# The second layer of a fused attention and MoE kernel in its loop's own order, with sums of token blocks on GpSimd

## The chip, the core and the metric

The kernel runs on one core of a Trainium2 chip. The metric is the device time of one execution in microseconds (us), as a median of several runs. The engines are TensorE (PE in the profile, its weight loads PEld), VectorE (DVE), ScalarE (ACT), GpSimd (POOL) and SyncE (SP), which here only issues transfers.

## The reference, cut to what matters

Two attentions in a row give x, 2304 tokens of 512 values. Then come two layers of matrix products:

```
h = x @ w_in                       # 512 -> 2048
x = (h * sigmoid(1.702 h)) @ w_out # 2048 -> 512          the first layer
p = probs / (probs.sum(-1) + 1e-9)
for e in range(4):                 # the second layer: 4 experts, w1[e] 512x1024, w2[e] 1024x512
    out += p[:, e] * (relu(x @ w1[e]) @ w2[e])
```

All inputs are float32. The kernel keeps the precision by splitting each operand into a rounded high part and the remainder, its low part, and adding three products of the four.

## The kernel before, in words

**Attention and the first layer** run first (up to 466 us of the profiled span). An order planned by hand covers the attention; the tail of the first layer, where the change begins, is issued by the framework's own scheduler. It steps through `moe` (eight token blocks j of 288 in the last pass, four steps c in each); after a step `moe_step` (the loop `while pos["m"] < len(moe) - CPP`) also advances what stands in the dictionary `beside` for it: there the operands of the second layer's first pair and first quad are made. PE's lines there are L500 and L528, VectorE's L520 (low part of a hidden block) and L553 (sum into the output block).

**The second layer** takes the tokens in three pairs of blocks of 2 x 384 (`NPAIR`, `TB`), and for each pair 16 **quads**: 4 experts times 4 slices of 256 hidden values, 48 quads in all. One quad computes relu(x @ w1 slice) for a whole pair by a seven-product scheme (`PRODUCTS`, L680) instead of eight products. Each product multiplies a sum of weight blocks (A11, S1 to S4, ...) by a sum of token blocks (B11, T1 to T4, ...), 6 matmuls of 128x384. What it needs:

- **Token operands**, once for a pair: `b_operand` (L593 to L615). T1 = B12-B11 and T2 = B22-T1 on VectorE (L592, L593), T3 = B22-B12 and T4 = B21-T2 on GpSimd (L597, L602), then for each of the seven names two high parts on ScalarE (L614) and two low parts, one on VectorE and one on GpSimd (L615). These take 10 buffers (28 thirds) and live through the pair's 16 quads.
- **Weight operands**, for each quad: `fetch_w1` (L622) and `fetch_w2` (L628) on SP; `w1_operand`: the sums S1 to S4 on VectorE (L649 to L653), then high parts on ScalarE and low parts on GpSimd (`split`, L153 and L154) in the order S2 S3, A11 A12, A22, S1 S4; `w2_operand` the same for two slices. Nine buffers for a quad: raw w1, the sums, four for w1's operands, raw w2, two for w2.

All of these come from one pool, `big`, with 29 buffers of equal size. A buffer is given in the order in which the kernel's text asks for it, when an older one has been read for the last time.

**A quad's loop** (the last loop of the kernel) has steps k = 0 to 7. Step k issues product k of quad n (`quad`), whose result VectorE adds up (L706, L710, L714, L715, L720) and ScalarE and VectorE turn into the two parts of a hidden block (`hidden`, L688 and L689); then one output tile of quad n-1 (`l2_second`: 6 matmuls of 128x512, L732, added up with the token's probability by VectorE, L743, in the first quad of a pair written by ScalarE, L741); then a step of the weight operands of quad n+1 and of w2 of quad n. At k = 5 the raw w2 of the next quad is asked for; in the last quad of a pair each step also makes one token operand of the next pair. An output tile that is finished is stored by SP (L747).

**What sets the order** in the kernel before: every engine runs its instructions in the order in which they stand in its queue. In the second layer and in the first layer's tail that order is not the text's but the framework scheduler's, which puts at the front what it takes to be ready first, the text's order deciding between ready ones.

Of the kernel before, what the change touches and what calls it, by code (L numbers as in the profile page):

```python
# [8 lines left out]
F32 = mybir.dt.float32  # L9
# [88 lines left out]
def packed_attention_moe_kernel(  # L98
# [13 lines left out]
    nc = tc.nc  # L112
    B, H, S, D = q.shape
# [11 lines left out]
    CPP = 4  # L125


    TB = 384
    NPAIR = NT // (2 * TB)
# [16 lines left out]
    def slot(shape, dt, name):  # L146
        return big.tile(shape, dt, tag="b", name=name)
# [17 lines left out]
    quads = [(i, e, c) for i in range(NPAIR) for e in range(NE) for c in range(w1.shape[2] // 256)]  # L165
# [413 lines left out]
    h2 = {}  # L579
    ACC2 = {}  # L580

    def b_operand(i):

        y = ACC[i]
        B = {f"B{r + 1}{b + 1}": y[:, 2 * r:2 * r + 2, b * TB:(b + 1) * TB] for r in range(2) for b in range(2)}
        parts = []
        one = two = None
        for n, name in enumerate(TOK):
            if name == "T2":
                one = slot([128, 2, TB], F32, "t1")  # L590
                two = slot([128, 2, TB], F32, "t2")
                nc.vector.tensor_sub(out=one, in0=B["B12"], in1=B["B11"])  # L592
                nc.vector.tensor_sub(out=two, in0=B["B22"], in1=one)  # L593
                src = two
            elif name == "T3":
                three = slot([128, 2, TB], F32, "t3")
                nc.gpsimd.tensor_sub(out=three, in0=B["B22"], in1=B["B12"])  # L597
                src = three
            elif name == "T1":
                src = one  # L600
            elif name == "T4":
                nc.gpsimd.tensor_sub(out=two, in0=B["B21"], in1=two)  # L602
                src = two
            else:
                src = B[name]
            for hl in range(2):
                for kk in range(2):
                    p = 4 * n + 2 * hl + kk
                    if p % 3 == 0:
                        parts.append(slot([128, 3, TB], F32R, "b"))  # L610
                    Bop[i, name, hl, kk] = parts[p // 3][:, p % 3, :]
            for kk in range(2):
                hi, lo = Bop[i, name, 0, kk], Bop[i, name, 1, kk]
                nc.scalar.copy(out=hi, in_=src[:, kk, :])  # L614
                (nc.vector, nc.gpsimd)[kk].tensor_sub(out=lo, in0=src[:, kk, :], in1=hi.bitcast(F32))  # L615
            yield

    def fetch_w1(n):
        if n < len(quads):
            i, e, c = quads[n]  # L620
            raw = raws["w1", n] = slot([128, KD, 256], F32, "raw1")
            nc.sync.dma_start(out=raw, in_=w1[e][:, c * 256:(c + 1) * 256].rearrange("(k p) f -> p k f", p=128))  # L622

    def fetch_w2(n):
        if n < len(quads):
            i, e, c = quads[n]
            raw = raws["w2", n] = slot([128, 2, 512], F32, "raw2")
            nc.sync.dma_start(out=raw, in_=w2[e][c * 256:(c + 1) * 256, :].rearrange("(c p) d -> p c d", p=128))  # L628
# [36 lines left out]
    def w2_operand(n):  # L665
        raw = raws.pop(("w2", n))
        for c in range(2):
            yield
            w = W2[n, c] = slot([128, 2, 512], F32R, "w2")
            split(w[:, 0, :], w[:, 1, :], raw[:, c, :], nc.gpsimd)  # L670
            yield
# [24 lines left out]
    def quad(n):  # L696

        for b in range(2):
            h2[n, b] = hp.tile([128, 2, 2, TB], F32R, tag="h", name=f"h{b}")
        ps = product(n, 0)  # L700
        P = f32_tile("p1")
        nc.scalar.copy(out=P, in_=ps)  # L702
        yield
        ps = product(n, 1)
        U = f32_tile("u")
        nc.vector.tensor_add(out=U, in0=ps, in1=P)  # L706
        yield
        ps = product(n, 2)
        UV = f32_tile("uv")
        nc.vector.tensor_add(out=UV, in0=ps, in1=U)  # L710
        yield
        ps = product(n, 3)
        C22 = f32_tile("c22")
        nc.vector.tensor_add(out=C22, in0=ps, in1=UV)  # L714
        nc.vector.tensor_add(out=U, in0=ps, in1=U)  # L715
        hidden(n, 1, 1, C22)
        yield
        for k, c, b, more in ((4, 0, 0, P), (5, 1, 0, UV), (6, 0, 1, U)):
            ps = product(n, k)
            nc.vector.tensor_add(out=more, in0=ps, in1=more)  # L720
            hidden(n, c, b, more)
            yield
# [33 lines left out]
    def norm_probs():  # L756
        nc.sync.dma_start(out=pr, in_=probs.rearrange("(t p) e -> p t e", p=128))
        nc.vector.reduce_sum(out=prs, in_=pr, axis=AX.X)
        nc.vector.tensor_scalar_add(prs, prs, 1e-9)
        nc.vector.reciprocal(out=prs, in_=prs)  # L760
        nc.vector.tensor_mul(out=pr, in0=pr, in1=prs.unsqueeze(2).to_broadcast([128, NT // 128, NE]))
# [4 lines left out]
    moe = [(packed_w, (0, 0), None)]  # L766
# [22 lines left out]
    pos = {"m": 0}  # L789
# [16 lines left out]
    def moe_step():  # L806
        fn, args, tag = moe[pos["m"]]
        pos["m"] += 1
        part = fn(*args)
        if part is not None:  # L810
            order.drain(part)
        due["n"] = max(due["n"], todo.get(tag, 0))
        if state["cvt"] < due["n"]:
            make_w()
        for part in beside.get(tag, ()):
            next(part, None)
# [56 lines left out]
    engines = {e.engine for e in (nc.tensor, nc.vector, nc.scalar, nc.gpsimd, nc.sync)}  # L873
    with tc.manual_schedule(engines=engines):
# [13 lines left out]
        for p in list(order.parts):  # L888
            order.finish(p)
    norm_probs()  # L890
    b_parts = {i: b_operand(i) for i in range(NPAIR)}
    last = n_pass1 - 1
    fetch_w1(0)
    fetch_w2(0)
    first = w1_operand(0)
    beside = {}
    for j in (6, 7):
        for c in range(CPP):
            beside["first", last, j - 1, c] = (b_parts[0], first)
    while pos["m"] < len(moe) - CPP:  # L900
        moe_step()
    per_pair = len(quads) // NPAIR

    for n in range(len(quads) + 1):
        none = iter(())
        now = quad(n) if n < len(quads) else none
        fetch_w1(n + 1)
        after = w1_operand(n + 1) if n + 1 < len(quads) else none
        w2_now = w2_operand(n) if n < len(quads) else none
        tiles = list(range(2 * TB // 128))  # L910
        for k in range(8):
            next(now, None)
            if k > 0:
                if n == 0:
                    if pos["m"] < len(moe):
                        moe_step()
                elif tiles:
                    l2_second(n - 1, tiles.pop(0))
            next(after, None)
            next(w2_now, None)  # L920
            if k == 5:
                fetch_w2(n + 1)
            if n % per_pair == per_pair - 1 and n // per_pair + 1 < NPAIR:
                next(b_parts[n // per_pair + 1], None)


# [28 lines left out]
```

## Time and profile before

| | |
|---|---|
| median of 3 runs | 1252.76 us (1251.65 to 1253.18) |
| the profiled execution, its own time | 1249.63 us |
| span in its profile | 1247.4 us |
| PE busy in the span | 1175.7 us, 94% |
| VectorE, ScalarE, GpSimd busy | 899.5, 523.6, 483.0 us |
| mean granted clock of TensorE | 0.967 |

The span is the time from the first to the last instruction; the execution's own time has 2.2 us more around it. In the profile "busy" is the time in which an engine works on an instruction; the square brackets at the end of a timeline row give the idle time of that engine just before it, and what ended it. In the windows' rows (x79) is a number of instructions, and PEclk is the granted share of TensorE's full clock.

### The profile page before, as it was taken

What the parts mean: (1) busy time and instruction counts of PE and PEld (TensorE: products, weight loads), DVE (VectorE), ACT (ScalarE), POOL (GpSimd) and SP (SyncE); (2) the same over time, 40 slices, a digit from 0 to 9 for tenths busy, and PEclk for the clock granted to TensorE, in tenths of its full rate; (3) what the DMA queues carried; (4) which work ended last, traced back from release to release, by engine and by line L of the source; (5) the groups of instructions that cost most, each with busy time, mean ns of one, the idle gap of its engine ahead of it and who ended that gap; (6) DMA issues with size and microseconds to landing.
All of it is one profiled execution on the core that took longest, in us unless ns stands there. A gap on an engine that the chain in (4) does not pass through costs nothing. (4 is left out here: it accounts for less than half of the span.)

```text
span 1247.4 us, 18269 instructions
## 1 busy us (share of the span) xinstructions
PE 1175.7 (94%) x6912; PEld 1062.0 (85%) x6912; DVE 899.5 (72%) x1652; ACT 523.6 (42%) x1152; POOL 483.0 (39%) x409
## 2 busy tenths in 40 slices
PE   5778788999999989999999989999999999999998
PEld 4467577999999989999999969999999789999997
DVE  4873678786875856777777876777778767777775
ACT  3567655444434634433333444333333353333321
POOL 1320023221120345544444664444444744444430
PEclk8779989999999989999999989999999899999999
DMA  8623321121110012222222132222221332222201
GB/s 234 177 76 82 85 66 54 51 69 52 51 35 18 1 51 69 68 68 69 68 68 68 34 118 69 68 68 68 68 69 41 95 119 68 68 68 68 68 18 51
DMA packets 90392, 87.46 MB, mean 70 GB/s; under 512 B 43968, under 2 KB 71616, under 8 KB 90304
## 3 DMA queue, kind: packets, MB, share of 16 engines
q1 hardware_dynamic: 90304, 86.30, 23.1%
q8 instruction: 54, 0.88, 0.3%
q14 instruction: 34, 0.28, 0.1%
HBM read 81.56 MB, written 4.72 MB: 69 GB/s over the span
## 5 line engine op out<-in xcount | busy, mean ns | idle before, releaser
L732 PE MATMUL ps_o<-w,h 128*128 128x512 f32 x1728 | 449.9, 396 | 9.7 <-ACT h L688 5.5
L680 PE MATMUL ps_p<-b,w 128*128 128x384 f32 x2016 | 402.8, 339 | 0.6 <-DVE o L743 0.6
L680 PEld LDWEIGHTS ps_p<-b,w 128*128 128x128 f32 x2016 | 362.8, 189 | 24.6 <-DVE o L743 0.9
L732 PEld LDWEIGHTS ps_o<-w,h 128*128 128x128 f32 x1728 | 323.4, 189 | 63.6 <-DVE h L689 7.2
L154 POOL TENSOR_TENSOR w<-raw,w 128x512 fp32r<-128x512 f32 x192 | 236.4, 1250 | 172.3 <-ACT w L153 170.5
L528 PE MATMUL ps_acc<-h,wout 128*128 128x288 f32 x1536 | 232.9, 300 | 6.1 <-DVE h L520 6.1
L528 PEld LDWEIGHTS ps_acc<-h,wout 128*128 128x128 f32 x1536 | 215.1, 191 | 10.0 <-DVE h L520 7.3
L743 DVE SCALAR_TENSOR_TENSOR o<-ps_o,pr,o 128x512 f32<-128x512 f32 x270 | 200.0, 741 | 5.1 <-PE ps_o L732 5.1
L154 POOL TENSOR_TENSOR w<-s,w 128x512 fp32r<-128x512 f32 x96 | 132.6, 1381 | 170.4 <-ACT w L153 170.4
L500 PE MATMUL ps_h<-a,pw 128*128 128x288 f32 x768 | 129.9, 305 | 19.1 <-ACT a L446 12.6
L153 ACT CAST w<-raw 128x512 fp32r<-128x512 f32 x192 | 106.9, 562 | 72.4 <-POOL w L154 48.0
L500 PEld LDWEIGHTS ps_h<-a,pw 128*128 128x128 f32 x768 | 113.6, 195 | 22.9 <-ACT a L446 13.4
L520 DVE TENSOR_TENSOR h<-g,h 128x288 fp32r<-128x288 f32 x128 | 73.4, 575 | 63.0 <-ACT g L517 62.0
L649 DVE TENSOR_TENSOR s<-raw 128x256 f32<-128x256 f32 x48 | 48.5, 1010 | 86.1 <-DMA raw<-in_moe_w_dram 69.8
L516 ACT ACTIVATE h<-ps_h 128x288 fp32r<-128x288 f32 x128 | 53.1, 415 | 96.5 <-PE ps_h L500 95.9
L688 ACT ACTIVATE h<-uv 128x384 fp32r<-128x384 f32 x48 | 25.2, 526 | 162.5 <-DVE uv L720 162.5
L706 DVE TENSOR_TENSOR u<-ps_p,p 128x384 f32<-128x384 f32 x48 | 26.7, 556 | 70.4 <-ACT p L702 67.2
L153 ACT CAST w<-s 128x512 fp32r<-128x512 f32 x96 | 59.1, 615 | 41.9 <-DVE s L650 19.2
L217 POOL TENSOR_SCALAR cvt<-cvt 128x512 uint32<-128x512 uint32 x32 | 23.9, 747 | 127.0 <-DVE cvt L214 108.4
L688 ACT ACTIVATE h<-c 128x384 fp32r<-128x384 f32 x48 | 25.2, 525 | 92.5 <-DVE c L714 92.5
L688 ACT ACTIVATE h<-p 128x384 fp32r<-128x384 f32 x48 | 25.2, 526 | 82.4 <-DVE p L720 82.4
L553 DVE TENSOR_TENSOR y<-ps_acc,y 128x288 f32<-128x288 f32 (+2 forms) x120 | 44.7, 388 | 11.2 <-PE ps_acc L528 11.0
(102 smaller groups left out, 1169.5 us busy)
## 6 DMA issues: line engine op xcount, KB each, us to landing
raw<-in_moe_w_dram SPq DMA_DIRECT2D x96, 512.0 KB, 3.9
raw<-in_moe_w_in_dram SPq DMA_DIRECT2D x16, 512.0 KB, 4.1
raw<-in_moe_w_out_dram SPq DMA_DIRECT2D x16, 512.0 KB, 3.8
kv<-in_k_dram SPq DMA_DIRECT2D x32, 144.0 KB, 3.3
q<-in_q_dram SPq DMA_DIRECT2D x32, 144.0 KB, 2.9
out_dram<-o SPq DMA_DIRECT2D x18, 256.0 KB, 2.0
kv<-in_v_dram SPq DMA_DIRECT2D x16, 144.0 KB, 3.0
kv<-in_v_dram SPq DMA_DIRECT2D x8, 288.0 KB, 3.5
```

What stands on the lines that cost most here:

```text
L153: nc.scalar.copy(out=hi, in_=src)
L154: eng.tensor_sub(out=lo, in0=src, in1=hi.bitcast(F32))
L500: nc.tensor.matmul(out=ps[:, :HS], lhsT=PW[a, b, g][:, wp, c * 128:(c + 1) * 128], rhs=A[b * UG + g][:, xp, s * HS:(s + 1) * HS], start=(m ...
L516: nc.scalar.activation(out=h[:, 0, :], in_=ps[:, :HS], func=AF.Gelu_apprx_sigmoid)
L520: nc.vector.tensor_sub(out=h[:, 1, :], in0=g32, in1=h[:, 0, :].bitcast(F32))
L528: nc.tensor.matmul(out=ps[:, :HS], lhsT=W["out", a, c][:, wp, t * 128:(t + 1) * 128], rhs=hid[a, j, c // 2][:, 2 * (c % 2) + hq, :], start ...
L553: nc.vector.tensor_add(out=dst, in0=src, in1=dst)
L649: nc.vector.tensor_add(out=s1, in0=Am["A21"], in1=Am["A22"])
L680: nc.tensor.matmul(out=ps, lhsT=Wop[n, a, wp, kk], rhs=Bop[i, b, xp, kk], start=(m == 0), stop=(m == 5),)
L688: nc.scalar.activation(out=h[:, 0, :], in_=src, func=AF.Relu)
L732: nc.tensor.matmul(out=ps, lhsT=h[:, c, hq, o:o + 128], rhs=W2[n, c][:, wp, :], start=(c == 0 and m == 0), stop=(c == 1 and m == 2),)
L743: nc.vector.scalar_tensor_tensor(out=acc, in0=ps, scalar=pr[:, tok, e:e + 1], in1=acc, op0=ALU.mult, op1=ALU.add,)
```

## The change

The four sums of token blocks become a generator of their own, `t_sums`, all on GpSimd and each in a buffer of its own; `b_operand` only reads them. For the first pair the steps in the first layer's tail at which sums, operands and the first quad's weights are advanced are moved: the sums beside token block 3, the weights beside 4 and 5, the operands beside 5 and 6 (before: operands and weights beside 5 and 6). For the other pairs the sums are taken in the last quad but one of the pair before (k = 0 to 3), and the operands in the last quad one step later than before (k = 1 to 7). The whole loop over quads, the last four steps of the first layer in quad 0 among it, stands in `tc.manual_schedule`: each engine issues its instructions in the order in which the text emits them.

```diff
+    Tsum = {}
+    def t_sums(i):
         y = ACC[i]
         B = {f"B{r + 1}{b + 1}": y[:, 2 * r:2 * r + 2, b * TB:(b + 1) * TB] for r in range(2) for b in range(2)}
+        for name, x, z in (("T1", "B12", "B11"), ("T2", "B22", "T1"), ("T4", "B21", "T2"), ("T3", "B22", "B12")):
+            B[name] = slot([128, 2, TB], F32, name)
+            nc.gpsimd.tensor_sub(out=B[name], in0=B[x], in1=B[z])
+            if name == "T3":
+                Tsum[i] = B
+            yield
+    def b_operand(i):
         parts = []
         for n, name in enumerate(TOK):
-            if name == "T2":
-                one = slot([128, 2, TB], F32, "t1")
-                two = slot([128, 2, TB], F32, "t2")
-                nc.vector.tensor_sub(out=one, in0=B["B12"], in1=B["B11"])
-                nc.vector.tensor_sub(out=two, in0=B["B22"], in1=one)
...
+            src = Tsum[i][name]
...
-    for j in (6, 7):
-        for c in range(CPP):
-            beside["first", last, j - 1, c] = (b_parts[0], first)
+    for c in range(CPP):
+        beside["first", last, 3, c] = (t_parts[0],)
+        beside["first", last, 4, c] = (first,)
+        beside["first", last, 5, c] = (b_parts[0], first)
+        beside["first", last, 6, c] = (b_parts[0],)
...
+    with tc.manual_schedule(engines=engines):
         for n in range(len(quads) + 1):
...
             for k in range(8):
...
-            if n % per_pair == per_pair - 1 and n // per_pair + 1 < NPAIR:
-                next(b_parts[n // per_pair + 1], None)
+                after_pair = n // per_pair + 1
+                if after_pair < NPAIR:
+                    if n % per_pair == per_pair - 2:
+                        next(t_parts[after_pair], None)
+                    if n % per_pair == per_pair - 1 and k > 0:
+                        next(b_parts[after_pair], None)
```

## Rows read from the trace of the kernel before

**Rows 1.** The page, busy time, share of the span and instructions of each engine.
```profile
PE 1175.7 (94%) x6912; PEld 1062.0 (85%) x6912; DVE 899.5 (72%) x1652; ACT 523.6 (42%) x1152; POOL 483.0 (39%) x409
```
**Rows 2.** Windows: length, busy PE, PEld, DVE, ACT, POOL, clock, DMA share, GB/s.
```profile
699.20:714.86 15.66, 15.66 (x79) 14.13 (x78) 13.46 (x19) 8.18 (x18) 12.60 (x11) 1.00 0.14 37
714.86:736.10 21.24, 18.04 (x79) 15.36 (x78) 12.62 (x24) 7.96 (x16) 14.04 (x12) 0.92 0.36 105
736.10:756.73 20.63, 17.97 (x80) 15.29 (x78) 15.14 (x26) 9.25 (x17) 9.74 (x8) 0.92 0.43 146
756.73:772.39 15.66, 15.66 (x80) 14.13 (x78) 10.88 (x18) 6.71 (x13) 7.38 (x6) 1.00 0.22 67
...
975.97:998.07 22.10, 19.32 (x79) 16.16 (x78) 14.38 (x25) 7.96 (x16) 14.69 (x12) 0.85 0.38 117
998.07:1015.79 17.72, 16.04 (x80) 13.96 (x79) 12.26 (x24) 9.04 (x17) 8.85 (x7) 1.00 0.45 148
```
**Rows 3.** Timeline of PE at the first change of pair: start, duration, what, idle before.
```profile
714.86 2.25 PE L680 MATMUL ps_p<-b,w 128*128 128x384 f32 x12
...
719.04 0.50 PE L732 MATMUL ps_o<-w,h 128*128 128x512 f32 x1 [1.47 <-DVE h L689]
```
**Rows 4.** Timeline of VectorE at the first change of pair.
```profile
695.14 2.22 DVE L689 SCALAR_TENSOR_TENSOR h<-p,h 128x384 fp32r<-128x384 f32 x1 [0.19 <-ACT h L688]
...
699.09 1.66 DVE L689 SCALAR_TENSOR_TENSOR h<-uv,h 128x384 fp32r<-128x384 f32 x1 [0.59 <-ACT h L688]
...
702.46 0.56 DVE L689 SCALAR_TENSOR_TENSOR h<-u,h 128x384 fp32r<-128x384 f32 x1 [0.59 <-ACT h L688]
...
716.76 0.43 DVE L649 TENSOR_TENSOR s<-raw 128x256 f32<-128x256 f32 x1 [1.78 <-DMA raw<-in_moe_w_dram]
```
**Rows 5.** Timeline of SP's queue at the first change of pair.
```profile
676.26 0.37 SPq L622 DMA_DIRECT2D raw<-in_moe_w_dram  x1
703.38 0.37 SPq L628 DMA_DIRECT2D raw<-in_moe_w_dram  x1
713.42 0.37 SPq L622 DMA_DIRECT2D raw<-in_moe_w_dram  x1
...
737.88 7.64 SPq L747 DMA_DIRECT2D out_dram<-o  x4
```
**Rows 6.** The page, DMA issues: the loads of w1 and w2, us to landing.
```profile
raw<-in_moe_w_dram SPq DMA_DIRECT2D x96, 512.0 KB, 3.9
```
**Rows 7.** Groups by line with shapes, whole run: busy us, mean ns of one, idle before.
```profile
L154 POOL TENSOR_TENSOR w<-raw,w 128x512 fp32r<-128x512 f32 x144 | 202.4, 1418 | 172.1 <-ACT w L153 170.2 <-PE ps_p L680 1.9
...
L153 ACT CAST w<-raw 128x512 fp32r<-128x512 f32 x144 | 87.8, 614 | 24.0 <-PE ps_p L680 15.7 <-DMA raw<-in_moe_w_dram 6.1 <-POOL w L154 2.1
...
L615 POOL TENSOR_TENSOR b<-t,b 128x384 fp32r<-128x384 f32 x12 | 13.7, 1142 | 24.7 <-PE ps_p L680 13.1 <-ACT b L614 6.1 <-DVE h L520 5.5
L741 ACT ACTIVATE o<-ps_o,pr 128x512 f32<-128x512 f32 x18 | 12.3, 681 | 0.5 <-PE ps_o L732 0.5
...
L615 DVE TENSOR_TENSOR b<-t,b 128x384 fp32r<-128x384 f32 x12 | 11.0, 919 | 0.0
...
L597 POOL TENSOR_TENSOR t<-y 128x768 f32<-128x768 f32 x3 | 5.9, 1951 | 0.0
...
L593 DVE TENSOR_TENSOR t<-y,t 128x768 f32<-128x768 f32 x3 | 2.8, 945 | 0.0
```
**Rows 8.** Timeline of GpSimd at the first change of pair.
```profile
695.10 1.85 POOL L602 TENSOR_TENSOR t<-y,t 128x768 f32<-128x768 f32 x1 [0.85 <-DVE b L615]
...
698.49 1.84 POOL L597 TENSOR_TENSOR t<-y 128x768 f32<-128x768 f32 x1
```
**Rows 9.** Windows in the first layer's last pass, columns as in rows 2.
```profile
400.00:410.00 10.00, 10.00 (x77) 10.00 (x77) 3.82 (x9) 2.85 (x8) 0.00 (x0) 1.00 0.01 2
440.00:450.00 10.00, 5.96 (x33) 5.50 (x32) 6.34 (x13) 5.41 (x14) 8.32 (x8) 0.78 0.18 54
450.00:460.00 10.00, 10.00 (x69) 10.00 (x68) 4.09 (x11) 2.35 (x7) 1.53 (x2) 0.88 0.19 52
```
**Rows 10.** Timeline of VectorE there.
```profile
444.79 0.47 DVE L649 TENSOR_TENSOR s<-raw 128x256 f32<-128x256 f32 x1 [1.80 <-DMA raw<-in_moe_w_dram]
```

More of the change, by code (lines that the diff above doesn't have):

```diff
@@ L580, in packed_attention_moe_kernel @@
     ACC2 = {}
-    def b_operand(i):
+    Tsum = {}
+    def t_sums(i):
         y = ACC[i]
         B = {f"B{r + 1}{b + 1}": y[:, 2 * r:2 * r + 2, b * TB:(b + 1) * TB] for r in range(2) for b in range(2)}
+        for name, x, z in (("T1", "B12", "B11"), ("T2", "B22", "T1"), ("T4", "B21", "T2"), ("T3", "B22", "B12")):
[5 more added lines that the diff above has]
+    def b_operand(i):
         parts = []
-        one = two = None
         for n, name in enumerate(TOK):
-            if name == "T2":
-                one = slot([128, 2, TB], F32, "t1")
-                two = slot([128, 2, TB], F32, "t2")
-                nc.vector.tensor_sub(out=one, in0=B["B12"], in1=B["B11"])
-                nc.vector.tensor_sub(out=two, in0=B["B22"], in1=one)
[L594 to L605, printed above, removed]
+            src = Tsum[i][name]
             for hl in range(2):
@@ L890, in packed_attention_moe_kernel @@
     norm_probs()
+    t_parts = {i: t_sums(i) for i in range(NPAIR)}
     b_parts = {i: b_operand(i) for i in range(NPAIR)}
@@ L902, in packed_attention_moe_kernel @@
     per_pair = len(quads) // NPAIR
[L904 to L922, printed above, removed]
-            if n % per_pair == per_pair - 1 and n // per_pair + 1 < NPAIR:
-                next(b_parts[n // per_pair + 1], None)
+    with tc.manual_schedule(engines=engines):
+        for n in range(len(quads) + 1):
+            none = iter(())
+            now = quad(n) if n < len(quads) else none
+            fetch_w1(n + 1)
+            after = w1_operand(n + 1) if n + 1 < len(quads) else none
+            w2_now = w2_operand(n) if n < len(quads) else none
+            tiles = list(range(2 * TB // 128))
+            for k in range(8):
+                next(now, None)
+                if k > 0:
+                    if n == 0:
+                        if pos["m"] < len(moe):
+                            moe_step()
+                    elif tiles:
+                        l2_second(n - 1, tiles.pop(0))
+                next(after, None)
+                next(w2_now, None)
+                if k == 5:
+                    fetch_w2(n + 1)
+                after_pair = n // per_pair + 1
[4 more added lines that the diff above has]
+                        next(b_parts[after_pair], None)
 _INS = ['q', 'k', 'v', 'p', 'moe_w_in', 'moe_w_out', 'moe2_domain_probs', 'moe2_w1', 'moe2_w2']
```

## The prediction

> **What bounds the kernel now.** I read the page's busy times first: PE works 94% of the span, nothing else above 85%, and that 85% is PE's own weight loads [rows 1]. So the question is where PE is not working. The windows answer it. I cut them at the first product of a quad, so that a row is one quad. A quad that goes well takes 15.66 us with PE busy all of it and the clock at 1.00; so do all others from the second quad on except the first two after each change of pair [rows 2]. Those four take 21.24, 20.63, 22.10 and 17.72 us: 81.69 - 4 x 15.66 = **19.05 us** lost, with the clock down to 0.92 and 0.85 in three of them [rows 2]. Everything that the change can win inside the second layer is in these four rows, since in the other quads no engine makes PE wait.
>
> What PE waits for there is the hidden block, 1.47 us at 719.04 [rows 3]; VectorE makes it late, and VectorE itself had stood 1.78 us at 716.76 for raw weights [rows 4]. The load is late because SP's queue sent nothing from 676.26 to 703.38, 27 us in which at 15.66 a quad three to four loads would go out [rows 5]. I put that down to the pool of 29 buffers: the scheduler lets the weights run more than a quad ahead, so all 29 are taken; then the next pair's ten operand buffers are asked for while the old ten live until their products in quad 15. The first load after the gap goes out when quad 15's first two products, begun at 699.20 [rows 2], have been through and free the old pair's first buffers. The trace does not show the pool, so this is my reading.
>
> A second loss lies in the first layer's tail: 33 and 69 matmuls in two 10 us windows where 77 go through undisturbed, (44 + 8) / 77 x 10 = **6.8 us**, with clocks of 0.78 and 0.88 [rows 9]. There too VectorE stands for raw weights, 1.80 us at 444.79 [rows 10], of a quad that is a whole quad away.
>
> **The change part by part.** *The loop's own order, clean quads.* PE's order stays the same (a product, an output tile, in turn). The other engines can no longer take work of a later step ahead. Weights are then made one quad ahead, not two. I count buffers: 10 token operands, the four weight operands of this quad and of the next in part, w2 of two quads, raw and sums: 22 to 23 of 29 in use at the worst step. So a raw load has six or more tiles' lead over the loop, more than half a quad, and lands after 3.9 us [rows 6]: no wait. VectorE's clean quad is 10.88 of 15.66 us [rows 2] plus three waits of 0.59 for ScalarE's half of a hidden block [rows 4], 12.7 in all: it fits in order. The tightest thing is A11 A12 of the next quad at k = 4. Product 4 ends 5 products and 3 tiles in; 15.66 us for 42 matmuls of 384 columns and 36 of 512 make a product 1.04 and a tile 1.39, so at 9.4 us (twelve matmuls of two products in one go, 2.25 with the last one's tail [rows 3], agree). Then VectorE's add and ScalarE's half (about 0.55 each, as 0.56 for the like [rows 4]), the cast 0.61 and GpSimd's 1.42 [rows 7]: 12.5, needed at 15.66. Slack 3.2 us. Price of the clean quads: 0. If that cover is gone, each microsecond past the slack costs 45 quads as much.
>
> *Sums on GpSimd in quad 14 (and 30).* Added: T1 and T2 at 1.95 us each, removed from VectorE 2 x 0.95; moved: T3 and T4 [rows 7]. GpSimd gets 7.38 [rows 2] + 4 x 1.95 = 15.2 of 15.66 us, and what is queued behind the sums are the low parts of quad 15's weights. VectorE pays too: while L602 ran at 695.10 a hidden part took 2.22 us, while L597 ran at 698.49 another took 1.66, against 0.56 [rows 4, 8]: 1.4 us for each sum that meets one. Four of them: 10.88 + 1.8 + 5.5 = 18.2, so VectorE leaves quad 14 some **2.5 us behind**. Bounds: 0 (no sum meets a VectorE instruction with both inputs in buffers) and 4 x 1.95.
>
> The Trainium skill, page SBUF — State Buffer, section Who interferes with whom, has GpSimd and a VectorE instruction with two SBUF inputs exclude each other for the whole instruction; the two rows agree, 2.22 and 1.66 us being the wait for the sum's end and 0.56 more. Its page Perfetto Trace Analysis, section Optimizing Scalar/DVE Operations, warns that moving work between these two engines might therefore not help; by that the two moved sums would cost VectorE up to 2 x 1.95 where they save 2 x 0.95, and the sum below would be some 2 us a pair worse.
>
> *Operands in quad 15 (and 31), a step later.* Seven low parts on VectorE at 0.92, seven on GpSimd at 1.14, 14 casts on ScalarE [rows 7]. VectorE: 10.88 + 1.8 + 6.4 = 19.1, **3.5 us more behind**, 6.0 in all. In the kernel before, the same quad had 13.46 us of VectorE and no sums of weights in it; they came after it, late [rows 2, 4]. GpSimd: 7.38 + 8.0 = 15.4 of 15.66. The step's delay lets an old buffer go free before a new one is taken; my count there is 26 to 28 of 29, so loads go on, if with a lead of one to three tiles.
>
> *What is late next.* At k = 4 of quad 15 VectorE is about 2.5 + 1.8 = 4.3 us behind, 1.1 past the slack: product 0 of quad 16 waits that long. S1 S4, cast at k = 6 with VectorE 6.0 behind, are there at 17.4 + 6.0 = 23.4, needed at 15.66 + 5.9 = 21.6: late by 1.8, of which the first wait has taken 1.1. With part of a slower clock after such a gap, as in rows 2, I take **2.2 us** a change of pair. Bounds 0 and 9.5, half of today's 19.05.
>
> *Stores in SP's order.* In quad 16 the six stores now stand in text order before the raw w1 of quad 18. The last waits for VectorE's last tile of that quad, then 0.37 + 0.37 to issue [rows 5] and 3.9 to land [rows 6], and the sums of weights stand at the head of VectorE's queue: 4.6 us idle. Half or more of it is covered, since quad 17's tiles are ScalarE's (a pair's first quad) and take six L743 off VectorE. I take 0.5 a change, between 0 and 2.
>
> *First pair.* VectorE loses 1.9 us of sums, GpSimd gains 3.9 where it is busy 8.32 of 10 us [rows 9]; the first quad's weights are asked for before its token operands, so the raw buffer for the next quad frees earlier. The sums of weights of quad 1 still may be put ahead of the first layer's work, as the first VectorE instructions of the ordered stretch. I take a gain of 3 between a gain of 6.8 and a loss of 3.
>
> **Sum** for the profiled execution: 1249.63 - 19.05 + 2 x 2.2 + 2 x 0.5 - 3 = 1233.0. That execution lies 3.1 us below the median of the runs shown, so **1236** for a median.
>
> **The rivals.** *Order is paid for at the change of pair* (0.17): GpSimd at 97% and VectorE 6 us behind, or more where GpSimd stalls it oftener, make PE wait 7 to 10 us a change, about as now. For it: the budgets above are all but full. Against: today's quad 15 holds 12.60 us of GpSimd and 13.46 of VectorE and PE is busy all of it [rows 2]. It decides from a lag of about 10 us on. Time 1243 to 1253 (1236 + 2 x 5 to 8).
>
> *Weights become the head of the queue in every quad* (0.10, slower). If the raw w1 gets its buffer only when the last weight operand before it is cast, at k = 6, then loading 3.9, VectorE's quad up to its last add (12.7 less about 1.3) and ScalarE's half and cast, 1.1, form one round of 16.4 us, 0.7 over 15.66: 45 x 0.7 = 32 us, 1268. It decides where fewer than some three of 29 buffers are free. Against: my count of 22 to 23.
>
> *The change does not do what it says* (0.08): the order is already the loop's where it matters, the sums hold four buffers instead of three and longer, and loads stop at a change as before: 1250 to 1258.
>
> **How the numbers follow.** Forecast 0.65, its own range 1226 to 1246. A measurement of this kernel tells 0.2%, 2.5 us, from no change. Faster: 0.65 + 0.08 of the first rival. Same: 0.06 of the first and 0.03 of the third. Slower: 0.03, 0.10 and 0.05. The range takes the forecast with its bounds (low: all of 19.05 and 6.8 won) and the first rival: 1225 to 1253.
>
> **What would show it.** Right: windows cut at products 0 of quads 14 to 18 and 30 to 34 at 16 to 18 us; SP's queue without a gap over 20 us; four L-lines of sums on GpSimd in quad 14 with hidden parts of about 2 us on VectorE beside them; clean quads at 15.66. Wrong: clean quads above 15.7 with VectorE idle for raw weights; or PE waiting at product 0 of quad 16 for weights by over 4 us; or a first layer's tail that loses more than 7 us.

## The result and the profile after

The changed kernel takes **1239.04 us** (median of 4 runs, 1236.59 to 1240.31) against 1252.2 (1250.73 to 1253.18): a ratio of 0.9892, 95% interval 0.9875 to 0.9908. The profiled execution took 1239.21 us, its span is 1237.4. All lines of the code stand six lower than before from the operand function on: products are now L674, output tiles L726, hidden blocks' low parts L683, loads L616 and L622, stores L741, the new sums L590.

The page's busy times (as in [rows 1]); GpSimd has 3.5 us more than before and VectorE 14.1, though six sums have moved from VectorE to GpSimd:

```profile
PE 1174.5 (95%) x6912; PEld 1059.5 (86%) x6912; DVE 913.6 (74%) x1646; ACT 522.9 (42%) x1152; POOL 486.5 (39%) x415
```

The windows cut at the first product of a quad, columns as in [rows 2]: quad 14, quads 16 to 18, quads 32 to 34. From the second quad to the last but one all others are 15.66 us, as before.

```profile
683.30:698.97 15.67, 15.67 (x80) 14.13 (x79) 14.63 (x18) 4.37 (x9) 14.91 (x9) 1.00 0.22 68
714.63:732.45 17.82, 16.49 (x80) 13.79 (x78) 15.88 (x26) 8.02 (x18) 12.01 (x10) 1.00 0.12 46
732.45:750.77 18.32, 17.59 (x79) 15.59 (x80) 10.49 (x21) 8.89 (x17) 8.54 (x7) 0.91 0.53 164
...
970.02:987.84 17.82, 16.48 (x80) 13.76 (x78) 15.89 (x26) 8.05 (x18) 12.02 (x10) 1.00 0.20 72
987.84:1004.74 16.90, 16.17 (x79) 13.99 (x79) 9.67 (x19) 7.87 (x15) 7.26 (x6) 1.00 0.52 172
1004.74:1021.51 16.77, 16.04 (x80) 14.18 (x80) 13.34 (x25) 8.03 (x17) 9.35 (x8) 1.00 0.21 64
```

Added up over 15.66 a quad: 2.16 + 2.66 + 0.02 + 2.16 + 1.24 + 1.11 = **9.35 us lost**, where the kernel before lost 19.05. I call this sum "the loss" below; every run is read by it, since it isn't touched by what the first layer does in one execution or another. It is touched by the clock, though. The loss holds time in which PE is idle and time in which PE works at a lower granted clock. The windows of quads 15 to 18 and of quads 31 to 34, before and after, columns as in [rows 2], tell the two apart:

```profile
699.20:772.39 73.19, 67.32 (x314) 58.91 (x312) 52.10 (x84) 32.10 (x64) 43.76 (x35) 0.95 0.30 94
960.31:1031.47 71.16, 66.70 (x314) 58.40 (x312) 50.44 (x84) 31.91 (x64) 43.51 (x35) 0.95 0.31 97
...
698.95:766.43 67.48, 65.42 (x313) 57.64 (x312) 52.66 (x89) 32.54 (x68) 39.20 (x32) 0.97 0.27 86
954.35:1021.50 67.15, 64.35 (x314) 56.05 (x312) 52.88 (x89) 32.36 (x68) 39.14 (x32) 1.00 0.27 87
```

Length less PE's busy time gives 10.3 us of idle PE before (5.87 + 4.46) and 4.9 after (2.06 + 2.80), and the clock rose from 0.95 to 0.97 and 1.00. I call the first "idle" below.

PE no longer waits for hidden blocks here, as it did in [rows 3]. It waits for weights, at product 0 of quads 16, 17 and 34 (timeline of PE; the rows for quads 32 and 33 repeat these waits):

```profile
715.33 2.03 PE L674 MATMUL ps_p<-b,w 128*128 128x384 f32 x10 [0.20 <-POOL w L154]
...
732.43 0.62 PE L674 MATMUL ps_p<-b,w 128*128 128x384 f32 x2 [1.12 <-ACT w L153]
733.78 3.04 PE L674 MATMUL ps_p<-b,w 128*128 128x384 f32 x10 [0.73 <-POOL w L154]
...
1006.08 2.01 PE L674 MATMUL ps_p<-b,w 128*128 128x384 f32 x10 [0.73 <-POOL w L154]
```

The weights of product 0 are A11 A12. Their cast needs raw weights only, but it stands in ScalarE's order behind the quad's hidden block, which waits for VectorE's add (timeline of ScalarE, two steps of quad 16):

```profile
731.35 0.52 ACT L682 ACTIVATE h<-p 128x384 fp32r<-128x384 f32 x1 [1.24 <-DVE p L714]
731.77 0.60 ACT L153 CAST w<-raw 128x512 fp32r<-128x512 f32 x1
```

So a late VectorE makes weights late that it has no part in. After the two waits around 733 the granted clock of quad 17's window is 0.91, and PE is busy 17.59 us with 15.66 us of work. Quad 33 has the same waits at a clock of 1.00 and takes 16.90 us, so 1.4 of quad 17's 18.32 us are the clock's.

SP's queue, timeline from quad 14 on (as in [rows 5]): the gap of 27 us in the queue is gone, the longest in these rows is 16.3. But what goes out at its end are stores: no load goes out from 710.46 to 735.85, 25.4 us. The six stores now stand ahead of the raw w1 of quad 18, at 738.13:

```profile
685.12 0.37 SPq L622 DMA_DIRECT2D raw<-in_moe_w_dram  x1
695.36 0.37 SPq L616 DMA_DIRECT2D raw<-in_moe_w_dram  x1
705.93 0.37 SPq L622 DMA_DIRECT2D raw<-in_moe_w_dram  x1
710.46 0.37 SPq L616 DMA_DIRECT2D raw<-in_moe_w_dram  x1
726.80 8.96 SPq L741 DMA_DIRECT2D out_dram<-o  x5
735.85 0.39 SPq L622 DMA_DIRECT2D raw<-in_moe_w_dram  x1
737.70 0.33 SPq L741 DMA_DIRECT2D out_dram<-o  x1
738.13 0.39 SPq L616 DMA_DIRECT2D raw<-in_moe_w_dram  x1
```

VectorE stands for that load, and as long, 5.19 us, for the same one of quad 34 (timeline of VectorE):

```profile
742.87 0.42 DVE L643 TENSOR_TENSOR s<-raw 128x256 f32<-128x256 f32 x1 [5.20 <-DMA raw<-in_moe_w_dram]
```

At the first change that costs nothing, since quad 17 is slow anyway (quad 18: 15.68); in runs 3, 7 and 9 below, whose quad 17 runs at full clock, quad 18 loses 1.1 us. At the second the wait at 1006.08 follows, and quad 33 is 1.11 us late at its end.

The first layer's tail, columns as in [rows 9], two of its windows. Where 33 matmuls went through from 440 to 450 there are 74 now, at full clock; the rest of the loss has moved ten microseconds ahead:

```profile
430.00:440.00 10.00, 7.12 (x52) 6.66 (x51) 9.97 (x13) 8.37 (x22) 8.65 (x8) 1.00 0.00 0
440.00:450.00 10.00, 9.75 (x74) 9.53 (x72) 9.96 (x17) 3.91 (x11) 6.46 (x5) 1.00 0.17 52
```

To compare executions I take the time from one matmul of the first layer, the 641st of L500 (near 405 us, where nothing is changed yet), to the first product of the second layer, both read from the trace's list of matmuls: 63.06 us before, 58.70 after. I call it "the tail". The clock has a part here too. As windows, columns as in [rows 2], before, after, and in run 3 below, which makes the same sums at the same steps:

```profile
403.25:466.31 63.06, 58.11 (x407) 56.89 (x406) 41.97 (x77) 30.15 (x76) 24.87 (x19) 0.95 0.07 20
407.36:466.06 58.70, 55.58 (x407) 54.36 (x406) 41.62 (x73) 27.40 (x70) 21.76 (x15) 1.00 0.04 11
409.00:469.78 60.78, 58.17 (x406) 56.98 (x405) 41.12 (x73) 27.49 (x70) 21.71 (x15) 0.94 0.04 11
```

At about the clock of before the tail takes 60.78 us, so about 2.1 of the 4.4 us are the clock's.

Accounts: 9.7 us from the changes of pair and 4.4 from the tail make 14.1; the medians differ by 13.2. Ahead of the tail the profiled execution after was 4.1 us later than the one before, all of it from before 225 us, in code that the change does not touch. The runs below were 0.3 to 5.8 us later there (run 5, with a smaller pool that the first layer draws on too, 10.6), so I count it as variation between executions.

### The profile page after: what moved, and what is told of

Its sections match the earlier page's. It is cut to its first block, busy times and chain, and to the rows that moved or that the text cites. A ratio compares the mean times of both kernels' runs of the same rounds, so it can differ in the third digit from the quotient of the medians.

```text
span 1237.4 us, 18457 instructions
## 1 busy us (share of the span) xinstructions
PE 1174.5 (95%) x6912; PEld 1059.5 (86%) x6912; DVE 913.6 (74%) x1646; ACT 522.9 (42%) x1152; POOL 486.5 (39%) x415
## 4 chain that ended last, share of the span: by engine, by line
PE 76%; DVE 4%; ACT 2%; issue 1%; POOL 0%; DVEq 0%
PE ps_o L726 30%; PE ps_p L674 27%; PE ps_acc L528 12%; PE ps_h L500 6%; DVE b L609 1%; PE ps_w L468 1%; ACT h L682 1%; DVE o L737 1%; ACT b L608 0%; DVE s L643 0%; DVE h L520 0%; ACT w L153 0%; DVE h L683 0%; POOL w L154 0%; DVE u L700 0%
## 5 line engine op out<-in xcount | busy, mean ns | idle before, releaser
L726 PE MATMUL ps_o<-w,h 128*128 128x512 f32 x1728 | 444.5, 393 | 0.0
L674 PE MATMUL ps_p<-b,w 128*128 128x384 f32 x2016 | 402.9, 338 | 4.9 <-POOL w L154 2.6
L674 PEld LDWEIGHTS ps_p<-b,w 128*128 128x128 f32 x2016 | 360.1, 188 | 32.1 <-POOL w L154 4.6
L726 PEld LDWEIGHTS ps_o<-w,h 128*128 128x128 f32 x1728 | 321.9, 188 | 50.2
L154 POOL TENSOR_TENSOR w<-raw,w 128x512 fp32r<-128x512 f32 x192 | 230.1, 1198 | 227.8 <-ACT w L153 222.9
L154 POOL TENSOR_TENSOR w<-s,w 128x512 fp32r<-128x512 f32 x96 | 125.2, 1304 | 164.3 <-ACT w L153 164.3
L500 PE MATMUL ps_h<-a,pw 128*128 128x288 f32 x768 | 129.0, 303 | 17.4 <-ACT a L446 12.6
L500 PEld LDWEIGHTS ps_h<-a,pw 128*128 128x128 f32 x768 | 112.5, 193 | 21.2 <-ACT a L446 13.4
L682 ACT ACTIVATE h<-u 128x384 fp32r<-128x384 f32 x48 | 25.2, 525 | 71.6 <-DVE u L714 71.6
L643 DVE TENSOR_TENSOR s<-raw 128x256 f32<-128x256 f32 x48 | 45.1, 941 | 10.4 <-DMA raw<-in_moe_w_dram 10.4
L517 ACT ACTIVATE g<-ps_h 128x288 f32<-128x288 f32 x128 | 52.6, 411 | 0.1
```

The lines of the kernel that those rows point to most:

```text
L154: eng.tensor_sub(out=lo, in0=src, in1=hi.bitcast(F32))
L500: nc.tensor.matmul(out=ps[:, :HS], lhsT=PW[a, b, g][:, wp, c * 128:(c + 1) * 128], rhs=A[b * UG + g][:, xp, s * HS:(s + 1) * HS], start=(m ...
L517: nc.scalar.activation(out=g32, in_=ps[:, :HS], func=AF.Gelu_apprx_sigmoid)
L643: nc.vector.tensor_add(out=s1, in0=Am["A21"], in1=Am["A22"])
L674: nc.tensor.matmul(out=ps, lhsT=Wop[n, a, wp, kk], rhs=Bop[i, b, xp, kk], start=(m == 0), stop=(m == 5),)
L682: nc.scalar.activation(out=h[:, 0, :], in_=src, func=AF.Relu)
```

## The experiments

Nearly all are read by the loss. Two of the edits work on each other, so a table stands first (us lost in the quads around the two changes of pair, and how much of it PE was idle; runs are numbered as they were made):

| sums and operands, in the text | the framework's order | the loop's own order |
|---|---|---|
| as before, all in quad 15 | 19.05, idle 10.3 (before) | 18.65, idle 11.0 (run 1) |
| sums in quad 14, operands a product later | 15.3, idle 10.7 (run 2) | 9.35, idle 4.9 (the change) |
| sums over quads 11 to 14, A11 A12 a step earlier | 24.3, idle 13.3 (run 11) | 0.90, idle 0.6 (run 8) |

So neither edit alone takes any waiting from PE, and the two together take more than half of it. The first column says where the text has the sums. The framework's scheduler runs them earlier than that: before the change already in quad 14 ([rows 8], and quad 15 begins at 699.20), in run 2 in quads 12 and 13. Under the loop's own order they run only when the text's turn comes, in run 1 the last one as late as quad 16. So it is the fixed order that needs the sums ahead in the text. Timeline of GpSimd, the first sum in run 2 (quad 13 begins at 665.28) and the last in run 1 (quad 16 begins at 720.38):

```profile
661.69 1.85 POOL L590 TENSOR_TENSOR T<-y 128x768 f32<-128x768 f32 x1 [3.74 <-PE ps_p L674]
...
724.26 1.85 POOL L602 TENSOR_TENSOR t<-y,t 128x768 f32<-128x768 f32 x1
```

**Run 1, the order alone.**

```diff
-    for n in range(len(quads) + 1):
+    with tc.manual_schedule(engines=engines):
+        for n in range(len(quads) + 1):
...
```

> The kernel before with one edit: the loop of the second layer is issued in its own order on every engine; the sums stay where they were (two on VectorE, two on GpSimd, all in quad 15), no operand is a product later, the first pair's hooks stay. Theory (the loss of 19.05 us at the two changes of pair came from weights loaded two quads ahead into a pool of 29 buffers, and the loop's own order removes it): no gap of SP's queue above 20 us ahead of quads 16 and 32; the quads 14 to 18 and 30 to 34 together lose 6 to 16 us over clean quads instead of 19 (more than the 9.4 us of the changed kernel, since VectorE has two more sums in quad 15); the time is 1240 to 1248 us. Rival (the sums taken ahead are what pays, the order is neutral): the quads after the changes lose 19 us as before or more, the time is 1250 to 1256 us.

Measured: 1251.04 us, ratio 0.9988 (0.9976 to 1.0); loss 18.65, idle 11.0. The rival's number, though not its reason. SP's queue still has a gap, 685.40 to 708.54, and yet no wait of PE in quads 15 and 16 comes from a raw load. What waits is one engine for another's sum, in strict order (ScalarE's cast of T3 for GpSimd, VectorE's low part for that cast, then PE):

```profile
714.39 0.93 ACT L614 CAST b<-t 128x384 fp32r<-128x384 f32 x2 [3.71 <-POOL t L597]
...
714.93 0.56 DVE L615 TENSOR_TENSOR b<-t,b 128x384 fp32r<-128x384 f32 x1 [3.41 <-ACT b L614]
...
720.38 0.86 PE L680 MATMUL ps_p<-b,w 128*128 128x384 f32 x2 [2.99 <-ACT w L153]
```

L597 had begun only at 712.52, behind two low parts on GpSimd. The order trades the old stall for a new one of the same size.

**Run 2, everything but the order.** The change without `tc.manual_schedule` around the loop.

> The changed kernel without the loop's own order: sums on GpSimd a quad ahead, operands a product later and the new hooks stay, the framework's scheduler orders the loop as it did before. Theory (order and pool): the gap of SP's queue ahead of quads 16 and 32 is back, the quads 14 to 18 and 30 to 34 lose 15 to 25 us in all, the time is 1245 to 1256 us. Rival (the sums ahead are what pays): the loss stays near 9 us and the time near 1239 us (1236 to 1242).

Measured: 1245.88 us, ratio 0.9954 (0.9936 to 0.9972); loss 15.3. PE waits for hidden blocks again, 7.5 us in 6 waits (9.8 in 8 before the change), and 3.1 us for sums into output tiles. SP's gap is back, 681.13 to 704.46. The windows of quads 15 to 18 and 31 to 34:

```profile
696.60:766.75 70.15, 64.34 (x313) 55.98 (x312) 48.39 (x82) 31.58 (x64) 44.40 (x36) 1.00 0.30 98
954.70:1025.12 70.42, 65.54 (x313) 57.45 (x312) 50.84 (x82) 31.72 (x64) 44.85 (x36) 0.98 0.31 98
```

PE is idle 10.7 us in them (5.81 + 4.88), as before. That this execution lost 3.7 us less is its clock, 1.00 and 0.98 instead of 0.95.

**Run 11, the same question with the best of the other edits** (run 8 without the order).

> The kernel with A11 A12 a step earlier and the sums spread over four quads, without the loop's own order. Theory (the loop's own order is needed as well: the framework's puts sums of weights of the quad after next ahead of hidden blocks, and their loads come late at the change of pair): the quads after the changes lose 10 to 18 us, the time is 1240 to 1248 us. Rival (order is neutral, as the first run's 18.65 against 19.05 us may be read; the earlier sums pay by themselves): they lose 1 to 5 us, the time is 1232 to 1236 us.

Measured: 1255.35 us, ratio 1.0022 (1.0011 to 1.0033); loss 24.3, beyond the theory's range, 13.3 of it idle and the rest at a clock of 0.93; as a whole it is slower than before. The waits of VectorE from 690 to 780 us (us in total, times, longest):

```profile
DVE s L643 <- DMA raw<-in_moe_w_dram: 10.9, 6, 3.1
DVE h L683 <- ACT h L682: 8.4, 7, 3.4
```

Its timeline at the worst place, with a row of ScalarE's that stands ahead of the hidden block in ScalarE's queue:

```profile
734.85 0.62 ACT L153 CAST w<-s 128x512 fp32r<-128x512 f32 x1 [3.33 <-POOL w L154]
...
735.93 1.32 DVE L683 SCALAR_TENSOR_TENSOR h<-c,h 128x384 fp32r<-128x384 f32 x1 [3.42 <-ACT h L682]
...
742.39 0.43 DVE L643 TENSOR_TENSOR s<-raw 128x256 f32<-128x256 f32 x1 [2.21 <-DMA raw<-in_moe_w_dram]
```

And PE's, which waits for the hidden block behind it:

```profile
743.90 1.65 PE L726 MATMUL ps_o<-w,h 128*128 128x512 f32 x3 [3.83 <-ACT h L682]
```

The framework's order puts weights of a later quad, their sums on VectorE and their casts on ScalarE, ahead of the parts of hidden blocks that PE needs next. As long as the raw weights are there this costs nothing; at a change of pair they are not. That is what [rows 4] showed at 716.76, and in runs 2 and 11 earlier sums did not heal it.

**Run 5, the pool of buffers.** Two fewer buffers in the kernel before: `bufs=27` for `bufs=29`.

> The kernel before with 27 instead of 29 buffers in the large pool, nothing else. Read by the quads, since the first layer draws on the same pool. Theory (before, the weights run two quads ahead and the pool of 29 runs out at the change of pair): clean quads stay 15.66 us, the gap in SP's loads ahead of quad 16 grows above its 27.1 us and the quads 15 to 18 and 31 to 34 lose 23 to 35 us in all instead of 19.05. Rival (the pool does not bind there; VectorE's own work at the change is what is late): the loss stays 18 to 20 us.

Measured: one run of 1248.93 us; the loss is 11.8 us, in quads 16, 17, 32 and 33. Neither side expected less. Idle is 8.0 us instead of 10.3; the rest of the difference is the clock, 0.98 and 1.00 over the two stretches instead of 0.95. The gap in SP's queue stays (688.83 to 710.82), and the load at its end still waited for a product of PE, 21.5 us. In the kernel before the same wait was 26.7 (waits of SP's queue from 655 to 765 us: in total, times, longest):

```profile
SPq L628 <- PE ps_p L680: 26.7, 1, 26.7
```

A raw load reads an input and writes a buffer, so what it waits for here is its buffer: the gap itself is the pool's, by the releaser that the profile names. But the loads run less far ahead (raw w1 of quad 16 goes out 17.3 us before quad 15 begins instead of 22.9), and from 698 to 765 us VectorE stands for raw weights 1.4 us in one wait, where it stood 5.7 us in four before. So two buffers fewer did not cost more, which speaks against the pool's size as what sets the loss; it is one execution.

**Run 6, a buffer more** (30, with 4 combination tiles instead of 6 to make room).

> The kernel before with one buffer more in the large pool (30), paid for with two fewer of the pool of combination tiles (4 instead of 6). Read by the quads. Theory (pool of 29): the gap in SP's loads ahead of quad 16 shrinks and the quads 15 to 18 and 31 to 34 lose 12 to 17 us instead of 19.05. Rival (the pool does not bind): the loss stays 18 to 20 us; if the fewer combination tiles bind, clean quads are longer than 15.66 us, and the run says nothing of the large pool.

Measured: 1278.37 us. From quad 6 on nearly all quads are 16.1 to 17.0 us long, with 35 waits of PE for ScalarE's half of a hidden block, so by the condition set ahead the run says nothing of the large pool. What a larger pool alone does stays open.

**Run 7, the delay of a product taken back.**

```diff
-                    if n % per_pair == per_pair - 1 and k > 0:
+                    if n % per_pair == per_pair - 1:
```

> The changed kernel without the delay: the operands of the next pair are again taken from the first step of quads 15 and 31, all else stays. Theory (what the order needs is that the sums are there before the operands' turn, so that no cast waits in order for a sum of another engine; the delay of a product is worth little): the quads after the changes lose 9 to 13 us, time 1238 to 1243 us. Rival (the delay is what pays along with the order): they lose 14 to 19 us as with the order alone (18.65), time 1245 to 1250 us.

Measured: 1238.26 us, ratio 0.9888 (0.987 to 0.9907); loss 9.14. In time the delay is worth nothing that can be measured; PE is idle 5.7 us instead of 4.9, at a clock of 1.00. So of the change it is in the main the order together with the early sums.

**Run 3, A11 A12 a step earlier.**

```diff
         yield
-        yield
         operand(("A11", "A12"), raw[:, :, :128].rearrange("p (o k) f -> p o k f", k=2))
         yield
+        yield
```

> The changed kernel with the split of A11 A12 one step earlier, in the step of the loop that was empty. Theory (what is left of the loss, 9.4 us, starts at product 0 of the quads 16 and 17, which waits for the split of A11 A12 that ScalarE and GpSimd run behind a late VectorE): with one product more of slack both waits (2 in each change of pair) go or shrink below 0.5 us; the loss falls to 2 to 6 us and the time to 1233 to 1237 us. Rival (VectorE's lag holds PE in some other way, through PSUM or the hidden blocks): the waits only move to another tile, the loss stays 8 to 11 us, the time 1238 to 1241 us. Second rival (a buffer held one product longer makes the pool bind again): SP loads late, the time is 1241 us or more.

Measured: 1235.54 us, ratio 0.9876 (0.9857 to 0.9895); loss 5.44 (the 6.55 in the expectation of run 8 below is a slip for it), idle 2.8, within the theory's range. Product 0 of quad 17 is on time (quad 16 takes 15.82 us), so the waits seen in the profile after are explained; part of the lag then shows at hidden blocks (0.63 us) and at product 0 of quad 18, behind the stores.

**Run 4, the sums on VectorE.** `nc.vector.tensor_sub` for `nc.gpsimd.tensor_sub` in the sums.

> The changed kernel with all four sums on VectorE instead of GpSimd, in the same steps of quads 14 and 30 (and in the first pair's hooks). Theory (a sum on GpSimd holds up the VectorE instructions beside it, 2.6 us in quad 14): the hidden blocks and the S sums in quad 14 are back at 0.56 and 0.42 us, a sum takes about 1.0 us, VectorE's busy time in quad 14 is 12.0 + 4 x 1.0 = 16.0 instead of 14.6, so VectorE falls further behind by 1 to 2 us; the loss at the changes of pair grows from 9.4 to 11 to 14 us, the time is 1240 to 1244 us. Rival (GpSimd's 14.9 us of 15.7 in quad 14 is what makes A11 A12 late, VectorE has room): the loss shrinks and the time is 1235 to 1238 us.

Measured: 1237.23 us, ratio 0.9894 (0.9872 to 0.9915); loss 9.45, as with GpSimd. VectorE's busy time in quad 14 is 14.89 us, not 16.0, because just as with GpSimd four instructions fewer of its own lie in the window: it is as far behind. Hidden blocks are back at 0.56, but two of the four sums are held up in turn (timeline of VectorE; a low part on GpSimd had begun 0.09 us ahead of the first of these and 0.58 ahead of the last):

```profile
680.76 2.05 DVE L590 TENSOR_TENSOR T<-y 128x768 f32<-128x768 f32 x1
...
684.53 0.94 DVE L590 TENSOR_TENSOR T<-y,T 128x768 f32<-128x768 f32 x1
...
689.66 1.53 DVE L590 TENSOR_TENSOR T<-y 128x768 f32<-128x768 f32 x1
```

With all four sums in one quad it does not matter for the changes of pair which engine takes them; spread over four quads it does (runs 8 and 10). The tail was 56.88 us here, the shortest seen until then.

**Run 8, both remedies:** A11 A12 earlier, and one sum a quad over four quads.

```diff
-                    if n % per_pair == per_pair - 2:
+                    if k == 0 and per_pair - 5 <= n % per_pair < per_pair - 1:
                         next(t_parts[after_pair], None)
```

> The changed kernel with the split of A11 A12 one step earlier (as in the third run) and the four sums one a quad over quads 11 to 14 (27 to 30), each in the quad's first step, instead of four in quad 14. Theory (what is left is VectorE's lag: four sums on GpSimd in quad 14 put it 2.5 us behind, the operands of quad 15 another 3.5): VectorE is about on time at the end of quad 14, the quads after the changes lose 0.5 to 4 us instead of 6.55, the time is 1229 to 1234 us. Rival (the lag of quad 14 does not add up with that of quad 15, what is left comes from the operands alone): they lose 6 to 7 us, the time is 1234 to 1237 us. Second rival (a sum holds its buffer up to three quads longer, and the pool binds): SP's loads come late and the time is 1238 us or more.

Measured: **1232.0 us**, ratio 0.9843 (0.9826 to 0.9859); loss 0.90. Quads 15 and 16, which hold the operands and their leftovers:

```profile
699.41:715.07 15.66, 15.66 (x80) 14.12 (x79) 13.50 (x24) 8.96 (x21) 12.35 (x10) 1.00 0.17 52
715.07:730.73 15.66, 15.66 (x80) 14.12 (x79) 14.31 (x22) 6.60 (x14) 10.88 (x9) 1.00 0.18 67
```

The lag was the whole of what was left, but for 0.83 us in quad 34 (the stores again: VectorE stands 5.3 us for its raw weights). That a sum holds its buffer for up to three quads more cost nothing that shows. SP's queue, with stores between, sends no load for 21.2 us here too, and quads 15 to 17 lose nothing:

```profile
712.85 0.37 SPq L616 DMA_DIRECT2D raw<-in_moe_w_dram  x1
...
734.07 0.39 SPq L622 DMA_DIRECT2D raw<-in_moe_w_dram  x1
```

So a gap in the loads is not by itself a loss.

**Run 9, the spread alone.**

> The changed kernel with the four sums one a quad over quads 11 to 14 (27 to 30), and the split of A11 A12 left where the change has it. Theory (the lag that VectorE brings out of quad 14 and the place of A11 A12 each carry a part of the 9.35 us): the quads after the changes lose 2 to 6 us, the time is 1232 to 1236 us. Rival (A11 A12's place alone decides; the spread matters only with it): they lose 8 to 10 us, 1237 to 1240 us.

Measured: 1233.41 us, ratio 0.9851 (0.9834 to 0.9868); loss 3.66. The lag out of quad 14 is the larger part (9.35 to 3.66), the place of A11 A12 the smaller (9.35 to 5.44); both differences hold the 1.4 us of slower clock that the change's execution had. In idle time they are nearer, 4.9 to 2.2 and 4.9 to 2.8.

**Run 10, run 8 with all sums on VectorE.**

> The kernel with A11 A12 a step earlier and the sums spread over four quads, with all sums on VectorE instead of GpSimd. Theory (a sum of 128x768 takes VectorE 0.95 us and GpSimd 1.85 to 2.05, and a quad has room for one on VectorE; in the first layer's tail GpSimd is the fuller one): the stretch from matmul 640 to the second layer takes 56.5 to 58.5 us as in the fourth run, the quads after the changes lose 0.5 to 2.5 us, the time is 1228 to 1232 us. Rival (VectorE is the tighter engine in the quads 11 to 15): they lose 3 us or more, the time is 1232 to 1236 us.

Measured: 1229.7 us, ratio 0.9825 (0.9811 to 0.9839); tail 56.84 as hoped, loss 3.88 as the rival had it. Both parts came out, and their net is a gain that the intervals don't separate from run 8.

**Run 12, mixed:** VectorE for the first pair's sums, GpSimd for the others.

> The kernel with A11 A12 a step earlier and the sums spread over four quads, the first pair's four sums on VectorE and the other pairs' on GpSimd. Theory (two separate terms that add up: in the first layer's tail GpSimd is the fuller engine, and sums on VectorE bring the stretch from matmul 640 to the second layer from 59.7 down to 56.9 us; at the changes of pair the spread sums on GpSimd lose 0.9 us where those on VectorE lose 3.9): stretch 56.5 to 57.5 us, loss 0.5 to 2 us, time 1225 to 1229.5 us. Rival (the two do not add up, the difference of 3 us between 0.9 and 3.9 is variation between executions): loss 3 to 4 us, time 1229 to 1232 us.

Measured: **1228.62 us**, ratio 0.9821 (0.98 to 0.9842); loss 1.29 as expected, but a tail of 58.40 instead of 56.5 to 57.5. Up to there this kernel runs the same instructions in the same order on every engine as run 10, and PE is idle 1.8 us in both: 56.84 at a clock of 1.00 and 58.40 at 0.97. The version beats both kernels; runs 8, 10 and 12 aren't told apart by their intervals.

The tails, for the term of the first pair, by the granted clock over the tail:

| | clock 0.94 to 0.95 | 0.97 | 1.00 |
|---|---|---|---|
| framework's order, old steps of the first pair | 63.06 (before), 63.04 (run 6) | 59.36 (run 5, 27 buffers) | |
| own order, old steps | | 61.47 (run 1) | |
| framework's order, new steps | | 60.06 (runs 2 and 11) | |
| own order, new steps | 60.78 (run 3) | 59.68 and 59.67 (runs 7, 8) | 58.70 (the change), 58.68 (run 9) |
| the same, first sums on VectorE | | 58.40 (run 12) | 56.88 and 56.84 (runs 4, 10) |

Executions in one cell agree within 0.1 us, so the variation in the tail of one kernel goes with the clock. The changed kernel with the old steps of the first pair was to be run as well and gave no time.

## Why the prediction was right in its number and half right in its reasons

**The loss it named was the one to win.** 9.7 of 19.05 us came back there, 5.5 of them idle time of PE and the rest in the main its clock, and runs 8 and 12 show that nearly all of it can. The place was read rightly from the windows, and so were the waits of PE for the hidden block and of VectorE for raw weights.

**"I put that down to the pool of 29 buffers": this step failed.** By that reading the order alone should have won most of the 19.05 us and fewer buffers should have cost more. The order alone won 0.4 and left PE as idle as before, and 27 buffers lost less than 29. What the runs show in its place is an order of instructions that is wrong when a load is late: work for a later quad ahead of a hidden block (before, runs 2 and 11), or a cast in front of everything that waits for a sum just issued on another engine (run 1). The gap in SP's queue is there in run 1 too, with another stall. That the gap is a wait for buffers the trace bears out (26.7 us for a product of PE); that the gap is the loss it does not, since run 8 has nearly as long a stretch without loads and loses 0.90. What a pool larger than 29 would do stays open.

**The prediction took the order as the gain and the sums ahead as its price.** The table shows that neither takes waiting from PE alone (idle 11.0 and 10.7 us against 10.3) and that together they do (4.9). The scheduler had run the sums early anyway; the fixed order takes that away, and the sums ahead in the text give it back. The sum came out near because it priced both at once, and that is luck as far as the reasons go.

**Clean quads at no cost:** right, 15.66 us in all of them.

**Sums in quad 14.** GpSimd 14.91 of 15.67 us (forecast 15.2), four sums of 1.84 to 2.05, four VectorE instructions beside them at 1.19 to 2.07 instead of 0.42 to 0.56: right. Timeline of GpSimd, the first two sums:

```profile
685.05 2.03 POOL L590 TENSOR_TENSOR T<-y 128x768 f32<-128x768 f32 x1
...
688.47 2.05 POOL L590 TENSOR_TENSOR T<-y,T 128x768 f32<-128x768 f32 x1
```

And of VectorE, the two that met them:

```profile
685.41 1.95 DVE L644 TENSOR_TENSOR s<-s,raw 128x256 f32<-128x256 f32 x1
...
688.74 2.07 DVE L647 TENSOR_TENSOR s<-raw,s 128x256 f32<-128x256 f32 x1
```

The Trainium skill's page Perfetto Trace Analysis, section Optimizing Scalar/DVE Operations, warns that moving work between these two engines might not help. Run 4 agrees for four sums in one quad: 9.45 against 9.35 us of loss, by either engine. Spread over four quads the engine matters: 0.90 on GpSimd (run 8), 3.88 on VectorE (run 10).

**"What is late next", 2.2 us a change: mis-sized.** With the stores it made 5.4 us for both changes; measured were 9.35. Product 0 of quad 16 does wait, but 0.20 us where 1.1 were forecast. And I let the lag end there, with S1 S4. It lasts through quad 16, where VectorE has 15.88 us of work, so product 0 of quad 17 waits as well (1.12 + 0.73 us), and S1 S4 never do. At the first change the slower clock adds 1.4 us in quad 17. The lags themselves were added up from too small a clean quad: the row with 10.88 us of VectorE is that of quad 18, with 18 instructions. In the changed kernel a clean quad has 22 and takes 12.02 us (window of quad 9), so each of the two lags, 2.5 and 3.5, should have been 1.1 larger:

```profile
605.00:620.66 15.66, 15.66 (x80) 14.12 (x79) 12.02 (x22) 5.55 (x12) 7.32 (x6) 1.00 0.23 69
```

**Stores, 0.5 a change:** VectorE stands 5.20 us (forecast 4.6). It cost nothing at the first change and 1.11 at the second, within the bounds of 0 and 2.

**First pair, a gain of 3:** the tail gained 4.4 in the profiled executions. At about the same clock it is 2.3 (63.06 against 60.78), so the term was near and the rest is the clock of this execution. By the tails at 0.97, 1.8 belong to the new steps and sums (61.47 against 59.67, both in the loop's own order) and 0.4 to the order (60.06 against 59.67). The pool's size moves the tail as well: run 5 has the old steps and the framework's order and takes 59.36. The profiled execution took 1239.21 us, 6.2 more than the 1233.0 of the sum. The two errors, 4.0 us more lost at the changes and 1.4 more gained in the tail, make 2.6 of them; the 4.1 us ahead of the tail make up the rest. That the median, 1239.04, lies only 3.0 above its forecast owes to the 3.1 us that were added for the median.

**The rivals.** Of the mechanism of the first (VectorE and GpSimd full at the change, PE waits) half came true, at 4.7 us a change instead of 7 to 10. The head of the queue in clean quads never showed. That the sums hold buffers and stop the loads did not show as a loss either: the 25.4 us without a load end behind the stores, and none of PE's waits at quads 16 and 17 is for a raw load.

## What to carry to other kernels

An order fixed by hand and work taken ahead are one edit: fix the order alone and every cast that waits for a fresh result of another engine now blocks what stands behind it; take work ahead in the text alone and a scheduler that ran it early anyway leaves the waits as they were. Spread extra work over the quads before a change instead of into the last one, and put a step that needs only loaded data ahead of the step in its queue that waits for another engine. Judge such edits by the lost time of the stretch, not by the median alone: runs 1 and 11 have nearly the time of before, and the table shows what each gives with its partner. And split that time into waiting and slower clock before comparing single executions: run 2 lost 3.7 us less than the kernel before with the same waiting.

## What the runs showed of the hardware

That a GpSimd subtraction holds up a VectorE instruction with two inputs in buffers was known from [rows 4, 8]. The runs add that it works the other way about too: in run 4 a sum of 0.94 us on VectorE took 2.05 and 1.53 us where a low part on GpSimd had begun first, so moving the sums back saved VectorE's hidden blocks and paid with the sums. And a wait of PE can cost more than its length: in the window after the waits at 732.43 and 733.78 (1.85 us) the granted clock was 0.91, while in the windows of quads 32 to 34, with waits of the same lengths, it stayed at 1.00; the two quads took 18.32 and 16.90 us. The same instructions of the tail took 56.84 us at 1.00 and 58.40 at 0.97. What decides between the two clocks the runs don't show.
